# One weight load of 128 rows, or eight loads of 16 rows each: the first transfer of a decode attention kernel

## The chip, the cores and the metric

The kernel runs on one core of a Trainium2 chip. The metric is the device time of one execution in microseconds (us). A core has a matrix engine (PE), a vector engine (DVE), a scalar engine (ACT), GpSimd (POOL) and a sync engine (SP), which work at the same time and wait for one another through semaphores. Data comes from the chip's main memory into the 128 rows (partitions) of the core's own memory through 16 DMA engines; SP and ACT each issue transfers into a queue of their own, and both queues are served by the same 16 DMA engines.

## The reference

```python
def _A_ref(x, k_cache, v_cache, wq, wo):          # B = 2, H = 16, Sk = 4096, Dh = 256, D = 448, all float32
    q = (x @ wq).reshape(B, Sq, H, Dh).transpose(0, 2, 1, 3)
    scores = einsum("bhqd,bhkd->bhqk", q, k_cache) * (Dh ** -0.5)
    p = softmax(scores)
    o = einsum("bhqk,bhkd->bhqd", p, v_cache)
    return o.transpose(0, 2, 1, 3).reshape(B, Sq, H * Dh) @ wo

def _B_ref(x, w1, b1, w2, b2):                    # D = 448, F = 1792
    h = x @ w1 + b1
    r = where(h > 0, h, 0)
    return (r * r) @ w2 + b2

g = sigmoid((x * gate_w).sum(-1, keepdims=True))
out = g * _A_ref(...) + (1 - g) * _B_ref(...)
```

One token for each of two sequences is decoded: attention over a cache of 4096 positions, a small feed-forward block beside it, and a gate that mixes the two. Nearly all the bytes are the two caches.

## The kernel before, in words

The work is cut into 16 rounds. A round is one sequence and two heads: a K tile and a V tile of 128 rows with 64 KB in each row. The two K tiles `kp0` and `kp1` are used in turn, and `vp` holds the V tile. For a round DVE multiplies K by the query, broadcast over the positions (`times_q`, L438), and sums each product (`row_sums`, L443); a maximum, the exponentials on ACT and the products with V on PE (`values`) follow. Rounds 0 to 11 run in hardware loops on PE, the last four are written out.

Every transfer goes through the helper `load` (L270), which gives it a semaphore by name and tells the flow which stretch of which tile it writes. The flow derives the waits from these stretches: a reader waits for the semaphores of the transfers that wrote what it reads. SP issues all large loads, in the order of the program text; an issue that has to wait for a buffer holds up everything behind it on SP.

The start matters here. SP issues, in this order: `wq` into the front of `vp` (L299), the K tile of round 0 (`load_k(0)`, L398), and then, once PE has read `wq`, `w1` into the same place, and the K tile of round 1. ACT issues four small loads (x, gate_w, b2, and b1 as 16 rows). When `wq` has landed, PE makes all the queries with `times_x` (56 matrix products into `po1`), ACT scales them into `qs`, PE and ACT spread the first two over the rows (`make_q`), and DVE can begin its first `times_q` when the K tile of round 0 is there as well. `wq` lies in memory so that each of the 128 rows of the tile gets one contiguous stretch of 57,344 bytes:

```python
wq_t = vp[:, :D * N // P]
load(SP, "wq", wq_t, wq.rearrange(by7, k=XR, s=2).rearrange("(p k) n -> p (k n)", k=XR), [place(vp, 0, D * N // P)])
```

## Time and profile before

| what | value |
|---|---|
| median of 3 runs | 677.41 us (677.40 to 677.64) |
| the profiled execution's own time | 677.56 us |
| its span, from the first to the last instruction | 676.2 us |
| DVE busy | 571.2 us (84% of the span) |
| PE busy | 251.1 us (37%) |
| bytes moved by DMA | 289.73 MB, 428 GB/s over the span |
| packets of SP's queue | 6624, which took 99.2% of the 16 DMA engines' time |

The times of single steps come from the profiled execution, counted from the start of its span; 1.36 us of its own time lie outside the span. It was 0.15 us above the median of the three runs, whose own spread is 0.24 us. In the stretches of the profile a packet's bytes are booked where the packet starts, so a stretch of a microsecond or two can show more than the engines can move or nothing at all; only long stretches give a rate.

### The profile page before, as it was taken

Reading aid. Unit: us, or ns where it says so; the run is one execution under the profiler, and the core shown is the slowest. Engines: PE = TensorE matmul, PEld = TensorE weight load, DVE = VectorE, ACT = ScalarE, POOL = GpSimd, SP = SyncE. Lnnn points to the kernel's source line nnn. Section 1 sums busy time; section 2 is a strip of 40 time slices with the busy share of each in tenths; the row PEclk is TensorE's granted clock in tenths of the full one; section 3 lists DMA queues with packets and bytes.
Section 4 is the critical chain, followed back from the end, with each engine's and each line's share of the span. In section 5 each row is a group of like instructions: output and inputs, shape, how many; then the busy total and the mean of one; then the engine's idle time right before and its main releaser. Section 6 shows DMA issues by size and latency. Waiting matters only on the chain.

```text
span 676.2 us, 3914 instructions
## 1 busy us (share of the span) xinstructions
PE 251.1 (37%) x1716; PEld 86.2 (13%) x1716; DVE 571.2 (84%) x147; ACT 43.0 (6%) x143; POOL 0.7 (0%) x6
## 2 busy tenths in 40 slices
PE   2612350402305751140505455050411480411597
PEld 1100210100001510010101411010100140100123
DVE  3069999999999895979979896897979899999930
ACT  0001000000100201010000201000010110000000
POOL 0000000000000000000000000000000000000000
PEclk9956585665758567585856578575575856565889
DMA  9999999999999999999999999999999999999997
GB/s 381 434 430 435 435 434 434 434 434 435 434 434 434 439 435 426 430 434 434 434 430 434 450 435 434 434 434 430 430 434 430 403 462 434 434 431 430 400 435 308
DMA packets 6695, 289.73 MB, mean 428 GB/s; under 512 B 790, under 2 KB 924, under 8 KB 1564
## 3 DMA queue, kind: packets, MB, share of 16 engines
q1 hardware_dynamic: 6624, 289.54, 99.2%
q8 instruction: 9, 0.15, 0.1%
q10 hardware_dynamic: 60, 0.02, 0.0%
q14 instruction: 2, 0.02, 0.0%
HBM read 289.56 MB, written 0.01 MB: 428 GB/s over the span
## 4 chain that ended last, share of the span: by engine, by line
DMA 43%; DVE 26%; PE 3%; SPq 0%; issue 0%; DVEq 0%
DMA kp<-in_A_k_cache_dram 26%; DVE s L443 13%; DVE kp L438 13%; DMA vp<-in_A_v_cache_dram 11%; DMA kp<-in_B_w_dram 6%; PE po L362 3%; SPq L270 0%; PE fin L362 0%; PE mt L362 0%; DVE shared L727 0%; DVE nb L465 0%; DVEq L155 0%
## 5 line engine op out<-in xcount | busy, mean ns | idle before, releaser
L438 DVE TENSOR_TENSOR kp<-kp,q 128x8192 f32<-128x8192 f32 (+2 forms) x34 | 278.2, 8183 | 49.4 <-DMA kp<-in_A_k_cache_dram 49.3
L443 DVE TENSOR_REDUCE s<-kp 128x32 f32<-128x8192 f32 x32 | 277.9, 8686 | 1.1
L362 PE MATMUL po<-vp,pw 128*16 128x512 f32 (+1 forms) x960 | 134.9, 724 | 229.5 <-PEq L153 208.7
L362 PEld LDWEIGHTS po<-vp,pw 128*16 128x16 f32 (+1 forms) x960 | 31.0, 110 | 330.1 <-issue 306.4
L362 PE MATMUL mt<-ident,m 128*64 128x64 f32 x64 | 7.3, 318 | 142.2 <-PEq L153 88.1
L362 PE MATMUL sm<-rl,shared 128*128 128x8 f32 (+1 forms) x120 | 24.4, 340 | 9.4 <-ACT shared L523 8.1
L362 PE MATMUL acc<-wo,oTw 128*2 128x448 f32 x48 | 24.8, 683 | 2.5 <-ACT oTw L532 2.5
L362 PEld LDWEIGHTS sm<-rl,shared 128*128 128x128 f32 x120 | 23.8, 303 | 11.6 <-DVE rl L496 4.6
L362 PEld LDWEIGHTS mt<-ident,m 128*64 128x64 f32 x64 | 4.8, 192 | 156.0 <-issue 99.8
L484 ACT ACTIVATE pw<-zero 128x128 f32<-128x128 f32 x12 | 3.7, 311 | 324.5 <-PE po L362 324.5
L472 ACT ACTIVATE pw<-s,nb 64x64 f32<-64x64 f32 x32 | 11.1, 348 | 169.8 <-DVE nb L465 169.6
L727 DVE COPY shared<-fin 128x112 f32<-128x112 f32 x1 | 0.3, 275 | 20.1 <-PE fin L362 20.1
L362 PE MATMUL po<-kp,pw 128*8 128x512 f32 x64 | 9.9, 779 | 6.9 <-DMA kp<-in_A_v_cache_dram 6.9
L362 PE MATMUL ph<-vp,xT 128*4 128x448 f32 x28 | 6.8, 648 | 15.3 <-DMA vp<-in_B_w_dram 15.3
L465 DVE TENSOR_REDUCE nb<-mt 128x1 f32<-128x64 f32 x16 | 3.6, 224 | 10.3 <-PE mt L362 10.3
L362 PE MATMUL pq<-qs,sel 128*64 128x256 f32 x48 | 12.3, 594 | 0.0
L362 PE MATMUL po<-vp,xT 128*4 128x512 f32 x56 | 9.1, 817 | 1.3 <-DMA vp<-in_A_wq_dram 1.3
L414 ACT ACTIVATE q<-pq 128x256 f32<-128x256 f32 x16 | 6.1, 384 | 21.6 <-PE pq L362 21.3
L494 DVE RECIPROCAL rc<-sm 128x8 f32<-128x8 f32 (+1 forms) x5 | 1.0, 196 | 7.7 <-PE sm L362 7.7
L523 ACT ACTIVATE shared<-po 128x512 f32<-128x512 f32 x12 | 6.5, 592 | 11.4 <-PE sm L362 11.4
L362 PEld LDWEIGHTS acc<-wo,oTw 128*2 128x2 f32 x48 | 4.5, 98 | 20.5 <-issue 17.8
L362 PE MATMUL ph<-kp,ones_pp 128*16 128x512 f32 x48 | 6.7, 593 | 0.0
(77 smaller groups left out, 77.2 us busy)
## 6 DMA issues: line engine op xcount, KB each, us to landing
vp<-in_A_wq_dram SPq DMA_DIRECT2D x1, 7168.0 KB, 19.7
wo<-in_A_wo_dram SPq DMA_DIRECT2D x3, 1792.0 KB, 46.5
vp<-in_A_v_cache_dram SPq DMA_DIRECT2D x1, 4096.0 KB, 24.2
vp<-in_B_w_dram SPq DMA_DIRECT2D x1, 3136.0 KB, 17.6
vp<-in_A_v_cache_dram SPq DMA_DIRECT2D x1, 3072.0 KB, 31.1
wo<-in_A_wo_dram SPq DMA_DIRECT2D x2, 896.0 KB, 33.9
kp<-in_B_w_dram SPq DMA_DIRECT2D x1, 1792.0 KB, 36.9
vp<-in_A_v_cache_dram SPq DMA_DIRECT2D x1, 1024.0 KB, 33.1
```

What stands on the lines that cost most here:

```text
L362: i = t_.matmul(out_, lhsT, rhs, start=start, stop=stop, skip_group_check=True)
L414: op(ACT, lambda: s_.activation(t, pq[:, :DH], AF.Copy), r=["pq"], w=[f"q{i % 3}"])
L438: vec(lambda: v_.tensor_tensor(kt, kt, q.unsqueeze(1).to_broadcast([P, hi - lo, DH]), op=ALU.mult), at + [f"q{i % 3}"], at)
L443: vec(lambda: v_.tensor_reduce(s[:, at], rows(t)[:, at, :], axis=AX.X, op=ALU.add), [place(t, half * HALF, (half + 1) * HALF)], [(f"s{i % ...
L465: vec(lambda: v_.tensor_reduce(nb, mt[:, :PH], axis=AX.X, op=ALU.max, negate=True), ["mt"], [f"nb{i % 2}"])
L472: op(ACT, lambda: s_.activation(pw[at, :, 2 * c:2 * c + 2], s[at].rearrange("p (m s) -> p m s", s=2), AF.Exp, bias=nb[at], accum_out=rs[at ...
L484: op(ACT, lambda: s_.activation(at, zero.unsqueeze(2).unsqueeze(3).to_broadcast([P, NK // 2, 2, 2]), AF.Copy), r=["zero"], w=[("pw0", 2 * ...
L494: vec(lambda: v_.reciprocal(c, sm[:, :B * n].rearrange("p (k b) -> p k b", b=B)), ["sm"], ["rc"])
L523: op(ACT, lambda s=s, lo=lo: s_.activation(o_w[:, s], pv[:, s, lo:lo + HJ // 2].unsqueeze(2).to_broadcast([P, HJ // 2, HG, HP]), AF.Copy), ...
L727: vec(lambda: v_.tensor_copy(y4, fin[:, :DQ]), ["fin"], [("shared", 0, DQ)])
```

## The change

The one load of `wq` becomes eight. Load number r (0 to 7) takes the rows r, r + 8, r + 16 and so on, 16 rows of 57,344 bytes. All eight count up one semaphore, `wq`, and the matrix products that read `wq` wait once, for the count of all eight. What each load writes is now kept under a name of its own (`wq0` to `wq7`), and the products still read the stretch of `vp` too, so `w1`, which goes into the same stretch, is still held back until they are done. The bytes, their place in the tile, the order of everything else on SP, and the products are the same.

```diff
+    WQ_STEP = 8
...
     by7 = "(r k) (s n) -> (r k s) n"
     wq_t = vp[:, :D * N // P]
-    load(SP, "wq", wq_t, wq.rearrange(by7, k=XR, s=2).rearrange("(p k) n -> p (k n)", k=XR), [place(vp, 0, D * N // P)])
+    wq_v = wq.rearrange(by7, k=XR, s=2).rearrange("(p k) n -> p (k n)", k=XR)
+    for r in range(WQ_STEP):
+        load(SP, "wq", wq_t[r:P:WQ_STEP, :], wq_v[r:P:WQ_STEP, :], [f"wq{r}"])
+    wq_at = [f"wq{r}" for r in range(WQ_STEP)] + [place(vp, 0, D * N // P)]
...
-    op(PE, times_x(po_t[1], wq_t, QB, NQ // 2), r=["xT", place(vp, 0, D * N // P)], w=["po1"])
+    op(PE, times_x(po_t[1], wq_t, QB, NQ // 2), r=["xT", *wq_at], w=["po1"])
```

## The prediction

> **What bounds the kernel now.** I read the slices first, then the queues, the chain, and last the rows of the first 60 us.

> ```profile
> DVE  3069999999999895979979896897979899999930
> PEclk9956585665758567585856578575575856565889
> DMA  9999999999999999999999999999999999999997
> GB/s 381 434 430 435 435 434 434 434 434 435 434 434 434 439 435 426 430 434 434 434 430 434 450 435 434 434 434 430 430 434 430 403 462 434 434 431 430 400 435 308
> q1 hardware_dynamic: 6624, 289.54, 99.2%
> DMA 43%; DVE 26%; PE 3%; SPq 0%; issue 0%; DVEq 0%
> ```

> The DMA engines are busy in every slice and move 434 GB/s in nearly all of them, whether wq, K, V or wo is on its way. SP's queue fills 99.2% of the time of the 16 engines. DVE has high shares too, but the chain gives 43% to DMA and 26% to DVE: DVE frees a K tile, the next loads queue behind what is already in flight, and DVE waits for them again. Long stretches of the middle say the same:

> ```profile
> 200.00:300.00 100.00, 45.16 (x258) 16.32 (x258) 89.11 (x18) 7.21 (x24) 0.00 (x0) 0.69 1.01 435
> 300.00:400.00 100.00, 38.10 (x202) 14.93 (x202) 89.80 (x21) 8.37 (x29) 0.00 (x0) 0.61 1.00 431
> 400.00:500.00 100.00, 30.57 (x216) 7.92 (x216) 87.00 (x16) 4.29 (x17) 0.00 (x0) 0.65 1.01 436
> ```

> The last two columns are the DMA share and GB/s: the queue has no gap in which a delay made at the start could be taken back, nor one into which time won there would vanish. Whatever the change does to the moment at which the first K tile has landed, it does to the end. So the question is only how long wq keeps the 16 engines. What happens there:

> ```profile
> 0.74 0.39 SPq L270 DMA_DIRECT2D vp<-in_A_wq_dram  x1
> 1.19 0.41 SPq L270 DMA_DIRECT2D kp<-in_A_k_cache_dram  x1
> 20.46 9.08 PE L362 MATMUL po<-vp,xT 128*4 128x512 f32 x56 [1.35 <-DMA vp<-in_A_wq_dram]
> 29.62 0.33 SPq L270 DMA_DIRECT2D vp<-in_B_w_dram  x1
> 32.11 0.38 ACT L414 ACTIVATE q<-pq 128x256 f32<-128x256 f32 x1 [0.75 <-PE pq L362]
> 39.87 8.69 DVE L438 TENSOR_TENSOR kp<-kp,q 128x8192 f32<-128x8192 f32 x1 [20.14 <-DMA kp<-in_A_k_cache_dram]
> vp<-in_A_wq_dram SPq DMA_DIRECT2D x1, 7168.0 KB, 19.7
> ```

> SP issues wq at 0.74 and the K tile right behind it. wq lands at 20.4, 19.7 us after its issue. The queries are ready at 32.49 (32.11 + 0.38), and DVE starts at 39.87, released by the K tile and not by the queries.

> **The data of wq, the term that decides.** 7168 KB are 7.340 MB; at 434 GB/s they take 16.91 us. One row is 56 KB, and one of 16 engines moves 434/16 = 27.1 GB/s, so a row takes one engine 2.12 us, eight rows one after the other. The short stretches show these waves (bytes are booked where a packet starts):

> ```profile
> 0.00:1.70 1.70, 0.00 (x0) 0.00 (x0) 0.71 (x3) 0.00 (x0) 0.70 (x6) 1.00 0.00 0
> 1.70:2.70 1.00, 0.00 (x0) 0.00 (x0) 0.94 (x3) 0.43 (x1) 0.00 (x0) 1.00 2.64 921
> 2.70:4.30 1.60, 0.00 (x0) 0.00 (x0) 1.56 (x10) 0.85 (x1) 0.00 (x0) 1.00 0.00 0
> 4.30:5.10 0.80, 0.12 (x1) 0.12 (x1) 0.63 (x3) 0.00 (x0) 0.00 (x0) 1.00 2.66 1147
> 5.10:6.40 1.30, 1.30 (x7) 1.30 (x7) 0.00 (x0) 0.00 (x0) 0.00 (x0) 1.00 0.00 0
> 6.40:7.20 0.80, 0.45 (x3) 0.36 (x2) 0.24 (x2) 0.00 (x0) 0.00 (x0) 1.00 2.68 1159
> ```

> Sixteen rows start between 1.7 and 2.7 (921 GB/s for 1 us is 16 times 57,344 bytes), the next sixteen from 4.3 on, the next from 6.4 on. So each engine works on one row at a time, and there is always one row of wq on each engine. The change keeps that: how a small transfer is spread can be counted in the first 20 us.

> ```profile
> q1 hardware_dynamic: 160, 8.39, 99.3%
> q10 hardware_dynamic: 44, 0.02, 0.5%
> ```

> ACT's queue, q10, has four loads in this stretch, three of 2 rows and b1 of 16 rows. If every engine in use gets one data packet and one closing packet, that makes 3 x 4 + 32 = 44, which is what is there. SP's queue has 128 rows of wq, 16 closing packets, and the first 16 rows of K: 160. A transfer of 16 rows therefore runs on all 16 engines with one row on each, and so will each of the eight.

> What changes is which sixteen rows are written at the same time. Before, the hardware divides 128 rows among the engines as it likes; afterwards the rows in flight together are r, r + 8, ..., r + 120. Whether these sixteen can be written at full speed no row of the trace shows, because every other large load has 128 rows. The bounds: at best the rate stays, 16.91 us. On the other side, if the rows go into the memory over paths that each serve several rows, and two of the sixteen share one, each engine gets half of its 27.1 GB/s: 4.23 us a row, 33.8 us for wq, +16.91 us. Four rows to a path would make it +50.7 us.

> I take the pairs, +16.91. The nearest evidence is the ceiling itself: 434 GB/s whether the source rows are K's 64 KB or wq's 56 KB, in all kinds of company, is a limit of fixed paths on the core's side rather than of the source, and rows at a regular distance of 8 are a narrow choice of rows. The trace fits that but doesn't prove it, hence the chances below.

> [...]

> **Seven more issues on SP, and the start.** The rows for issues that follow one another, and for the shortest one:

> ```profile
> 631.98 1.29 SPq L270 DMA_DIRECT2D vp<-in_A_v_cache_dram  x3
> 633.31 8.01 SPq L270 DMA_DIRECT2D kp<-in_B_w_dram  x4
> 1.33 0.25 ACTq L270 DMA_DIRECT2D kp<-in_gate_w_dram  x1
> ```

> Three issues in a row take 1.29 us, 0.43 each. Seven more move the K issue from 1.19 to about 4.2 (7 x 0.43 = 3.0). K's first rows are needed when wq's last have gone, near 19; 14 us of queued wq hide this, and without that cover it would cost the 3.0. Nor does an engine wait for its next row: load r is issued by about 0.74 + 0.43 r, and its wave begins at about 1.7 + 2.1 r at the earliest. In the tail four issues took 8.01 us, so SP can be held up by a long queue; but there, three pieces of V and several earlier loads lay ahead of them, and here at most eight closing packets per engine are added to eight rows. I count nothing.

> A smaller first load can only start sooner. The bounds: its issue may take 0.25 us in place of 0.39 (0.14), and the first wave took from 1.7 to 4.3, 2.6 in place of 2.1 us (0.5 if an engine no longer waits for other rows' descriptors). So 0 to 0.64 us are won; I take 0.3, because the first rows also have to come a first time.

> Each engine closes eight loads in place of one: seven packets more. ACT's 44 packets took 0.5% of 16 x 20 us, 36 ns each, with the small data packets among them: 0 to 0.25 us, I take 0.1, that is, nearer to the rows where a large packet follows at once.

> **Waits.** There is no new one. The eight loads share a semaphore, PE waits once, and ACT's and SP's own waits stay. What PE does behind wq is hidden now: queries are ready 7.4 us before DVE is released by K (32.49 against 39.87), and w1, issued at 29.62, has 10 us until K has left the queue. If wq is late, K is late by the same amount, so both covers move along. b1 and its product stand before the wq products in PE's order:

> ```profile
> 18.35 0.77 PE L362 MATMUL ph<-kp 16*128 16x112 f32 x2 [2.63 <-DMA kp<-in_B_b_dram]
> L362 PE MATMUL po<-vp,xT x56: 592/787/1057, 20.5 to 29.0; 128*4 128x512 f32 x56
> ```

> b1 is released at 18.35 between wq's packets; with waves twice as long it is there by 1.7 + 2 x 16.65 = 35.0 at the latest, and wq by 20.4 + 16.9 = 37.3: still in front. A lower clock would stretch the 56 products: the same product takes 592 to 1057 ns, so 9.08 us would become at most 9.08 x 1057/787 = 12.2, 3.1 more, inside the 7.4.

> **The sum.** In the profiled execution 677.56 + 16.91 - 0.3 + 0.1 = 694.3. It lay 0.15 above the median of the runs, which gives 694.1; since the gain at the start is uncertain where the first wave itself is slowed, I leave the two small terms out: 677.41 + 16.91 = 694.3. The case's own range has as its ends -1.0 (the 0.64, and some 0.4 of overlap where waves of different loads meet) and +1.2 (closings 0.25, and up to half of a 2.12 us row lost where the last wave passes over to K): 693.3 to 695.5. The smallest difference that a measurement of this kernel can tell from none I put at 0.2%, 1.35 us.

> **The rivals.** First, not slower: the order in flight is the old one. If an engine already worked through eight neighbouring rows, engine e on 8e to 8e + 7, then the sixteen rows in flight were always r, r + 8, ..., and the change repeats them exactly; or the paths serve any sixteen rows alike. For it speaks that the engines' 2.1 us per row stays the same through all eight waves; against it that nothing shows which rows these are. Its price is the start and the closings alone: 677.41 - 0.3 + 0.1 = 677.2, between 676.8 (-0.64) and 677.7 (+0.25). It decides from the second wave on: if that begins by 4.3 and the third 2.1 us later, this is the case. Chance 0.26, nearly all of it within 0.2%, for 0.64 is less than 1.35; 0.04 of it for a gain larger than any row suggests.

> Second, the pair shares unevenly: one engine of a pair runs at full rate through its first four rows (8.46 us) and the other is held back; then, if rows 4 to 7 of a block have other paths than rows 0 to 3, they no longer meet. The cost is half, 8.46 us: 685.9. For it speaks that the engines are not in step now (the starts of a wave are spread over about a microsecond); against it, that the spread stays that small and no engine gets ahead. Chance 0.07.

> Third, four rows to a path: 677.4 + 50.7 = 728.1. Against it: the sixteen rows are spread over the whole memory, from r to r + 120. Chance 0.03.

> Fourth, the change doesn't do what it says: a load of 16 rows uses fewer engines. The count of b1's packets speaks against it. With half of the engines and full rate, wq would take twice as long too, 694.3, unless loads run side by side. Chance 0.02, slower.

> **How the numbers follow.** Pairs at half rate 0.62, uneven 0.07, four to a path 0.03, fewer engines 0.02: slower by over 0.2% 0.74. No collision 0.26, of which 0.22 within 0.2% and 0.04 faster. The likeliest case gives 694.3. Its own range holds only about 0.6, so the range has to reach to the other end, the case without collision, whose low end is 676.8; I put 676.7 and 695.5, and the uneven case lies inside.

> **What would show it.** If I am right, the windows of the first 40 us show waves every 4.2 us in place of 2.1, about 217 GB/s over the stretch of wq, wq landing near 37, DVE's first multiplication near 56.8 in place of 39.87, and from there the same 434 GB/s and the same chain, shifted by 17 us. SP's issues of wq would still be 0.4 us apart. PE would reach its wait for wq later, behind b1, and lose nothing of its own. I am wrong if the third wave starts at 6.4 as before: then rows eight apart don't meet, and only the start counts. I am wrong in another way if wq takes 34 us but DVE starts less than 16 us later, or if a gap in the DMA row swallows part of it.

## The result, and the profile after

The changed kernel takes 696.60 us (median of 5 runs, 696.35 to 696.84) against 677.41 for the kernel before (5 runs beside it, 677.40 to 677.67): ratio 1.0282, 95% interval 1.0270 to 1.0293, or 19.2 us more. The forecast was 694.3 within 676.7 to 695.5. The direction and the halved rate came out; the size lies 1.1 us above the range.

The profiled execution of the changed kernel took 696.60 us, with a span of 695.2. First the slices and queues of its page:

```profile
DVE  3006999999999899697979899597979989999930
DMA  9989999999999999999999999999999999999997
GB/s 212 211 362 426 442 453 426 422 430 427 456 434 426 409 459 434 430 422 434 437 445 430 405 444 453 430 426 434 430 445 434 430 423 441 437 423 434 407 434 312
q1 hardware_dynamic: 6736, 289.54, 99.2%
DMA 42%; DVE 25%; PE 3%; SPq 0%; issue 0%; DVEq 0%
```

The bytes are the same; 112 packets are new (7 on each of 16 engines, as many as seven more closings each). The DMA engines are as busy as before, but in the first two slices (17.4 us each) they move 212 and 211 GB/s where 381 and 434 stood. From the fourth slice on the rate is the old one, and the shares of the chain are nearly the same. Now the first steps, from the order of time, and the waves of wq (us, busy time of the engines, clock, DMA share, GB/s in the last column):

```profile
0.73 5.08 SPq L271 DMA_DIRECT2D vp<-in_A_wq_dram  x8
5.86 0.58 SPq L271 DMA_DIRECT2D kp<-in_A_k_cache_dram  x1
13.22 0.76 PE L366 MATMUL ph<-kp 16*128 16x112 f32 x2 [1.47 <-DMA kp<-in_B_b_dram]
39.47 8.23 PE L366 MATMUL po<-vp,xT 128*4 128x512 f32 x56 [25.49 <-DMA vp<-in_A_wq_dram]
50.25 0.38 ACT L418 ACTIVATE q<-pq 128x256 f32<-128x256 f32 x1 [0.75 <-PE pq L366]
58.78 8.69 DVE L442 TENSOR_TENSOR kp<-kp,q 128x8192 f32<-128x8192 f32 x1 [44.19 <-DMA kp<-in_A_k_cache_dram]
```

```profile
0.00:2.10 2.10, 0.00 (x0) 0.00 (x0) 1.11 (x3) 0.00 (x0) 0.70 (x6) 1.00 0.01 2
2.10:5.50 3.40, 0.53 (x3) 0.53 (x3) 2.72 (x13) 1.28 (x1) 0.00 (x0) 1.00 1.26 270
10.00:14.50 4.50, 2.52 (x5) 0.66 (x5) 0.61 (x3) 0.00 (x0) 0.00 (x0) 1.00 1.00 206
14.50:19.00 4.50, 0.00 (x0) 0.00 (x0) 0.10 (x1) 0.00 (x0) 0.00 (x0) 1.00 0.99 204
19.00:23.30 4.30, 0.00 (x0) 0.00 (x0) 0.00 (x0) 0.00 (x0) 0.00 (x0) 1.00 1.00 213
23.30:27.80 4.50, 0.00 (x0) 0.00 (x0) 0.00 (x0) 0.00 (x0) 0.00 (x0) 1.00 1.00 204
32.30:36.80 4.50, 0.00 (x0) 0.00 (x0) 0.00 (x0) 0.00 (x0) 0.00 (x0) 1.00 0.99 204
40.00:57.00 17.00, 9.00 (x64) 1.78 (x56) 0.00 (x0) 1.36 (x3) 0.00 (x0) 0.91 1.00 432
```

Each of these waves is sixteen rows, and it now takes 4.3 to 4.5 us in place of 2.1 (the packets themselves: 2.116 us before; after, a median of 4.43 to 4.47 in six of the eight waves and 4.29 in the first and the fifth), although the DMA share is full. wq is there at 39.47 in place of 20.46, DVE starts at 58.78 in place of 39.87: 18.9 us later. The end of the span is 19.0 later. So all of the loss arises while wq is on its way, and none of it is taken back: the queries are ready at 50.63, 8.2 us before DVE can use them.

### The profile page after: what moved, and what is told of

Same layout as the page of the kernel before. It is cut to its first block, busy times and chain, and to the rows that moved or that the text cites. A ratio compares the mean times of both kernels' runs of the same rounds, so it can differ in the third digit from the quotient of the medians.

```text
span 695.2 us, 3921 instructions
## 1 busy us (share of the span) xinstructions
PE 253.3 (36%) x1716; PEld 86.6 (12%) x1716; DVE 571.2 (82%) x147; ACT 42.9 (6%) x143; POOL 0.7 (0%) x6
## 3 DMA queue, kind: packets, MB, share of 16 engines
q1 hardware_dynamic: 6736, 289.54, 99.2%
## 4 chain that ended last, share of the span: by engine, by line
DMA 42%; DVE 25%; PE 3%; SPq 0%; issue 0%; DVEq 0%
DMA kp<-in_A_k_cache_dram 26%; DVE s L447 13%; DVE kp L442 12%; DMA vp<-in_A_v_cache_dram 11%; DMA kp<-in_B_w_dram 6%; PE po L366 3%; SPq L271 0%; PE fin L366 0%; PE mt L366 0%; DVE shared L731 0%; DVE nb L469 0%; DVEq L155 0%
## 5 line engine op out<-in xcount | busy, mean ns | idle before, releaser
L366 PE MATMUL po<-vp,pw 128*16 128x512 f32 (+1 forms) x960 | 136.7, 733 | 228.2 <-PEq L153 206.5
L366 PE MATMUL acc<-wo,oTw 128*2 128x448 f32 x48 | 25.6, 702 | 2.5 <-ACT oTw L536 2.5
L366 PE MATMUL po<-vp,xT 128*4 128x512 f32 x56 | 8.2, 751 | 25.5 <-DMA vp<-in_A_wq_dram 25.5
L418 ACT ACTIVATE q<-pq 128x256 f32<-128x256 f32 x16 | 6.1, 383 | 20.7 <-PE pq L366 20.4
## 6 DMA issues: line engine op xcount, KB each, us to landing
wo<-in_A_wo_dram SPq DMA_DIRECT2D x2, 896.0 KB, 33.9
vp<-in_A_v_cache_dram SPq DMA_DIRECT2D x1, 1024.0 KB, 33.9
```

What stands on the lines that cost most here:

```text
L366: i = t_.matmul(out_, lhsT, rhs, start=start, stop=stop, skip_group_check=True)
L418: op(ACT, lambda: s_.activation(t, pq[:, :DH], AF.Copy), r=["pq"], w=[f"q{i % 3}"])
```

## The experiments

The theory on trial is a supposition: the 128 rows are written over 16 paths, and a path carries about what one engine can bring, so that two engines on one path each run at half rate. No record names a path; whether there are such groups of rows, and which rows are in one, only the rates below can say. The rivals: every load costs something of its own; the source rows, 448 KB apart, are read slowly; loads of 16 rows are slow whatever their rows. The experiments keep all else as in the change and replace its loop of loads.

**Eight loads of all rows, an eighth of the columns in each.**

```diff
-        load(SP, "wq", wq_t[r:P:WQ_STEP, :], wq_v[r:P:WQ_STEP, :], [f"wq{r}"])
+        load(SP, "wq", wq_t[:, r * WL:(r + 1) * WL], wq_v[:, r * WL:(r + 1) * WL], [f"wq{r}"])    # WL = 1792
```

> Eight loads of wq as in the change, with the same bytes and the same issues on SP, but each takes all 128 rows and an eighth of their columns (7,168 bytes of each row). Shared write paths (the rows in flight decide): as fast as the kernel before, 677.4 within 1 us, wq landed near 20.5, first DVE multiplication near 40. Number of loads (every load costs something of its own): as slow as the change, near 696.

677.96 us against 677.61, ratio 1.0005 (0.9996 to 1.0014). From its order of time:

```profile
0.74 4.22 SPq L271 DMA_DIRECT2D vp<-in_A_wq_dram  x8
40.14 8.69 DVE L443 TENSOR_TENSOR kp<-kp,q 128x8192 f32<-128x8192 f32 x1 [27.83 <-DMA kp<-in_A_k_cache_dram]
```

Eight issues take SP 4.22 us and DVE starts 0.27 later than before: the number of loads, their size of 896 KB and the later issue of K together cost a few tenths of a microsecond.

**Sixteen neighbouring rows in a load.**

```diff
-        load(SP, "wq", wq_t[r:P:WQ_STEP, :], wq_v[r:P:WQ_STEP, :], [f"wq{r}"])
+        load(SP, "wq", wq_t[r * WB:(r + 1) * WB, :], wq_v[r * WB:(r + 1) * WB, :], [f"wq{r}"])    # WB = 16
```

> Eight loads of 16 rows, but of 16 neighbouring rows each (16r to 16r + 15). [...] Number of loads: as the change, 696. Source rows too far apart: the sixteen source rows in flight are now neighbours, so about 677.

725.69 us, ratio 1.0708 (1.0691 to 1.0724), +48.1. Three of its waves, in windows:

```profile
16.30:24.50 8.20, 1.65 (x2) 0.08 (x2) 0.00 (x0) 0.00 (x0) 0.00 (x0) 1.00 1.01 113
24.50:32.60 8.10, 0.77 (x2) 0.50 (x2) 0.54 (x2) 0.00 (x0) 0.00 (x0) 1.00 1.01 113
32.60:40.80 8.20, 0.00 (x0) 0.00 (x0) 0.00 (x0) 0.00 (x0) 0.00 (x0) 1.00 1.00 112
```

A wave takes 8.16 us, nearly four times the 2.12. Same bytes, same number of loads, and source rows side by side, which should have helped if their distance were the cause: which rows are written together decides. The price is that of four rows to a path, a little under the 728.1 us that the prediction's third rival puts on it. An estimate from these rates, with four paths here and eight in the change: 112.5/4 = 28.1 GB/s for each of the four, against 204/8 = 25.5 for each of the eight, so that four engines on a path do not lose what a pair loses.

**The rows of the change, read from neighbouring source rows.**

```diff
-        load(SP, "wq", wq_t[r:P:WQ_STEP, :], wq_v[r:P:WQ_STEP, :], [f"wq{r}"])
+        load(SP, "wq", wq_t[r:P:WQ_STEP, :], wq_v[r * WB:(r + 1) * WB, :], [f"wq{r}"])
```

> The eight loads of the change write the same rows r, r + 8, ..., but read sixteen neighbouring source rows each (16r to 16r + 15), so wq lies in the tile in another order and the queries come out of permuted weights. Shared write paths alone: as the change, 4.47 us a row, 696.6. The distance of the source rows alone: 677. If pairs halve the rate and the source distance adds the 6% by which a row was slower than half rate (4.47 against 4.23): 4.23 us a row, 694.5.

696.16 us, ratio 1.0274 (1.0258 to 1.0290), rows of 4.25 to 4.47 us after the first wave, as in the change. One wave:

```profile
23.45:27.95 4.50, 0.00 (x0) 0.00 (x0) 0.00 (x0) 0.00 (x0) 0.00 (x0) 1.00 0.99 204
```

The source has no part in it that can be told (the time is 0.4 us below the change's), neither in the half rate nor in the 6% beyond it.

**Two loads, rows 0 to 63 and 64 to 127.**

```diff
-    for r in range(WQ_STEP):
-        load(SP, "wq", wq_t[r:P:WQ_STEP, :], wq_v[r:P:WQ_STEP, :], [f"wq{r}"])
+    for r in range(2):
+        load(SP, "wq", wq_t[r * PH:(r + 1) * PH, :], wq_v[r * PH:(r + 1) * PH, :], [f"wq{r}"])    # PH = 64
```

> Two loads of wq, rows 0 to 63 and rows 64 to 127. Shared write paths: each half reaches 8 of 16 paths, 4.2 to 4.5 us a row, 694 to 697. Number of loads: an eighth of the change's effect or less, 678 to 680. Small loads of 16 rows being slow in themselves: 677.

696.56 us, ratio 1.0281 (1.0265 to 1.0297). Two loads cost as much as eight, with rows of 4.25 to 4.48 us. One wave:

```profile
14.70:19.20 4.50, 0.00 (x0) 0.00 (x0) 0.00 (x0) 0.00 (x0) 0.00 (x0) 1.00 1.00 205
```

A load of 3.5 MiB to one half of the rows gave 205 GB/s in its steady waves against 434 before: a ratio of 0.47, a little below one half.

**Four loads of 32 rows, and two of 64, spread over the whole memory.**

```diff
+    for r in range(4):
+        load(SP, "wq", wq_t[r:P:4, :], wq_v[r:P:4, :], [f"wq{r}"])     # the other kernel: range(2), r:P:2
```

> Four loads of 32 rows, every fourth row in one (r, r + 4, ...). Each load reaches all 16 paths with two rows each, and every engine gets two rows. Shared write paths, engines dealt neighbouring entries of the list (rows r + 8e, then r + 8e + 4): the sixteen rows in flight are again eight apart, 4.47 us a row, 696. Shared write paths, engines dealt one path each, as the full rate of the 128-row load suggests: 2.12 us a row, 677.5. What counts is the paths that a load reaches as a whole, whatever is in flight: 677.5.

> Two loads of 64 rows, every second row in one (r, r + 2, ...). All 16 paths with four rows each, four rows for every engine. Engines dealt neighbouring entries (rows r + 8e, + 2, + 4, + 6): rows in flight eight apart again, 4.47 us a row, 696. Engines dealt one path each, or only the reach of the whole load counting: 677.5.

678.01 and 678.10 us, ratios 1.0005 (0.9996 to 1.0015) and 1.0006 (0.9996 to 1.0015). The second to fourth wave of the loads of 32 rows:

```profile
4.80:6.95 2.15, 1.86 (x8) 1.77 (x8) 0.13 (x1) 0.00 (x0) 0.00 (x0) 1.00 1.00 428
6.95:9.10 2.15, 0.00 (x0) 0.00 (x0) 1.47 (x9) 0.20 (x1) 0.00 (x0) 1.00 1.01 431
9.10:11.25 2.15, 1.64 (x4) 0.58 (x4) 0.35 (x3) 0.00 (x0) 0.00 (x0) 1.00 0.99 427
```

A load needn't have 128 rows: these two ran at full rate, 427 to 431 GB/s in these waves and 428 to 430 in the same ones of the loads of 64 rows. If the rows in flight decide, their rows were also dealt to the engines so that those in flight didn't meet, for dealing neighbouring entries would have put r + 8e together again and cost the 4.47 us a row of the change. The runs show the rate; the dealing is inferred from it.

**Sixteen rows with fewer meetings.**

```diff
+    for r in range(7):
+        load(SP, "wq", wq_t[r:r + 106:7, :], wq_v[r:r + 106:7, :], [f"wq{r}"])
+    load(SP, "wq", wq_t[112:P, :], wq_v[112:P, :], ["wq7"])
```

> Seven loads of 16 rows, every seventh row in one (r to r + 105), and one load of the rows 112 to 127. Shared write paths: in a load only two to four of sixteen rows meet another on their path, so most engines go on at 2.1 us a row and get out of step; worked out path by path, the slowest engine takes 25.4 to 26.2 us (the last load, four rows to a path, is most of the loss), +8.5 to +9.3: 686 to 687. Loads of 16 rows slow whatever their rows: 696.

695.68 us, ratio 1.0264 (1.0247 to 1.0281): a miss of 9 us. Its waves, one window each from load 2 to load 7:

```profile
5.70:9.94 4.24, 2.24 (x9) 1.64 (x9) 1.72 (x10) 0.20 (x1) 0.00 (x0) 1.00 1.00 217
9.94:14.10 4.16, 1.83 (x4) 0.49 (x2) 0.54 (x2) 0.00 (x0) 0.00 (x0) 1.00 1.02 222
14.10:17.12 3.02, 0.00 (x0) 0.00 (x0) 0.00 (x0) 0.00 (x0) 0.00 (x0) 1.00 0.96 304
17.12:20.06 2.94, 0.00 (x0) 0.00 (x0) 0.00 (x0) 0.00 (x0) 0.00 (x0) 1.00 1.05 312
20.06:23.68 3.62, 0.00 (x0) 0.00 (x0) 0.00 (x0) 0.00 (x0) 0.00 (x0) 1.00 1.09 253
23.68:27.80 4.12, 0.00 (x0) 0.00 (x0) 0.00 (x0) 0.00 (x0) 0.00 (x0) 1.00 1.02 223
```

Which rows share a path can be worked out from the rates. Sixteen groups of eight rows, the four rows 4m to 4m + 3 and the four that lie 32 away in the same half of the memory, put four rows in flight on a path in the blocks (8.16 us a row), two in the change (4.43 to 4.47) and in the pairs close to each other (4.47, below), and one in the loads of 8 rows without pairs (2.12, below). One half of the memory has eight of the sixteen groups, and went at half rate (205 GB/s). Of all groupings by four of the seven bits of the row number this is the only one that gives these rates; it is a fit to them, and no record shows a path itself.

By this grouping, loads 1 to 3, 6 and 7 have two pairs of rows on a shared path, loads 4 and 5 one pair. The waves follow it: 3.6 to 4.2 us with two pairs (loads 2, 3, 6 and 7), about 3 with one. But the twelve rows that by the grouping meet nobody were slow as well: in load 3 all sixteen packets took 4.00 to 4.19 us; in load 4 two took 4.21 and 4.22 and the rest 2.39 to 3.01. So by the grouping a crowded path held up the other engines too. That the engines work independently of one another was the wrong part of this expectation; through what they are coupled, none of the runs shows.

**Pairs of rows close to each other.**

```diff
+        lo, hi = 32 * (r // 2) + r % 2, 32 * (r // 2 + 1)
+        load(SP, "wq", wq_t[lo:hi:2, :], wq_v[lo:hi:2, :], [f"wq{r}"])
```

> Eight loads of 16 rows, every second row of a block of 32 (0, 2, ..., 30 first). Again eight paths with two rows each, but the two that meet are two rows apart and not 32 apart as in the change. The extra 6% (4.47 us a row against twice 2.116 = 4.23) due to the distance of the two rows on a path: 4.08 (half of the 8.156 that four neighbouring rows took) to 4.23 us, 693.1 to 694.3. Due to two engines sharing, whatever the rows: 4.47, 696.5.

696.78 us, ratio 1.0283 (1.0266 to 1.0300), again 4.47 us a row. One wave:

```profile
23.70:28.20 4.50, 0.00 (x0) 0.00 (x0) 0.00 (x0) 0.00 (x0) 0.00 (x0) 1.00 1.00 204
```

Whether the two rows that share a path by the grouping lie 2 apart, as here, or 32, as in the change, makes no difference to the 6%: 4.47 us against 4.43 to 4.47.

**Loads of 8 rows: four pairs, and no pair.**

```diff
+    for r in range(16):
+        load(SP, "wq", wq_t[r:P:16, :], wq_v[r:P:16, :], [f"wq{r}"])       # four pairs
...
+        lo, hi = 32 * (r // 4) + r % 4, 32 * (r // 4 + 1)
+        load(SP, "wq", wq_t[lo:hi:4, :], wq_v[lo:hi:4, :], [f"wq{r}"])     # no pair
```

> Sixteen loads of 8 rows, every sixteenth row in one (r, r + 16, ...), so that eight engines work and their rows meet in four pairs, in place of sixteen engines and eight pairs. The 6% by which a pair was slower than half rate belongs to any two engines on one path: 4.47 us a row, 16 rows one after the other 71.5 us, +54.6, about 732. It belongs to eight pairs at once: 4.1 to 4.25 us a row, 66 to 68 us, +49 to +51, about 727. If loads of 8 rows were dealt to other engines in turn, half of these times or less.

> Sixteen loads of 8 rows, every fourth row of a block of 32 (0, 4, ..., 28 first), so that each of the eight rows has a path of its own. Shared write paths: 2.12 us a row although the load is smaller than any of the others, 16 rows on each of eight engines 33.9 us, +16.9, about 694.5; engines dealt in turn: 677.5. Small loads slow in themselves: 4.2 us a row or more, +51 and over.

746.46 us (ratio 1.1017, 1.0985 to 1.1049) and 710.51 us (1.0486, 1.0456 to 1.0517), the first above every expected time, the second between two of them (694.5 for shared paths, some 728 for small loads slow in themselves). The windows of the kernel without pairs show why:

```profile
4.60:6.80 2.20, 1.82 (x8) 1.78 (x8) 0.32 (x2) 0.00 (x0) 0.00 (x0) 1.00 0.51 213
9.00:11.20 2.20, 2.20 (x5) 0.69 (x6) 0.16 (x1) 0.00 (x0) 0.00 (x0) 1.00 0.48 209
13.30:20.20 6.90, 0.00 (x0) 0.00 (x0) 0.00 (x0) 0.00 (x0) 0.00 (x0) 1.00 1.13 427
20.20:46.10 25.90, 0.00 (x0) 0.00 (x0) 0.00 (x0) 0.00 (x0) 0.00 (x0) 1.00 1.00 207
52.40:72.20 19.80, 9.78 (x64) 1.94 (x64) 0.00 (x0) 1.36 (x3) 0.00 (x0) 0.80 0.73 306
```

At first half of the engines work (share 0.5) and bring 209 to 213 GB/s, 2.12 us a row: these loads of only 8 rows, none of which meet by the grouping, ran at full rate per engine. At 13.8 the first rows of K, issued at 11.64, start on the eight idle engines. While wq writes rows 0 to 63, both together move 427 by the window; a share of 1.13 says that rows which end later are counted in, and at a share of 1 it is 378. From 20.2 on wq writes rows 64 to 127, and now all 16 engines together move 207: wq's rows take 4.45 us, K's 64 KB rows 5.1 in place of 2.42, until those eight engines are done with K. Then wq is back at 2.12 us. From this it is inferred that K's rows on those engines were rows 64 to 127, and that rows of different loads meet on a path just as rows of one load do; no record names the row that an engine writes. The rest of the extra time is K itself, whose other half still had to go through the engines that wq had kept (0.73 of DMA share from 52.4 to 72.2).

In the kernel with pairs a load of wq by the grouping uses four paths, two of them for rows from 64 on, and only on these two a third row, one of K's, can join. Yet in loads 6 and 7 all eight rows of wq took 6.35 us, three times 2.12 (5.1 to 6.4 over loads 3 to 11), and all eight rows of K beside them 7.2 to 7.3, three times 2.42:

```profile
33.00:39.30 6.30, 0.00 (x0) 0.00 (x0) 0.00 (x0) 0.00 (x0) 0.00 (x0) 1.00 0.73 105
```

At a share of 1 the 105 GB/s are 144, a third of 434: every engine went at the pace that three rows on one path would give, as in the step of seven every engine was near the pace of a pair (4.00 to 4.19 us in load 3). Before K starts and after its share is done there, wq's rows take 4.40 to 4.47 us (loads 2, 14 and 15): with four pairs the loss beyond half rate is 4 to 6%, about that of eight pairs.

**A step of five rows.**

```diff
+    for r in range(15):
+        lo = 40 * (r // 5) + r % 5
+        load(SP, "wq", wq_t[lo:lo + 36:5, :], wq_v[lo:lo + 36:5, :], [f"wq{r}"])
+    load(SP, "wq", wq_t[120:P, :], wq_v[120:P, :], ["wq15"])
```

> Fifteen loads of 8 rows, every fifth row of a block of 40, and one of the rows 120 to 127. Worked out by the bits of the row number, loads 1 to 5 and 11 to 15 have one or two pairs on a path among their eight rows, loads 6 to 10 none. If only the rows that meet are slow, the other four to six rows of a load keep 2.12 us. If a crowded path holds up every engine (as the step of seven suggested, where two pairs slowed all sixteen to 4.15 and one pair the rest to 2.4 to 3.0), the other rows of loads 1 to 5 and 11 to 15 take 2.4 to 4.2 us, and those of loads 6 to 10 are back at 2.12. In time 705 to 722, with the last load, four rows to a path, near 8.2 us of it.

726.01 us, ratio 1.0715 (1.0684 to 1.0746), above the range. Here too K was under way on the other engines, from 12.5 us on. In the middle of the loads without pairs all engines together moved about half of 434:

```profile
20.00:37.00 17.00, 0.00 (x0) 0.00 (x0) 0.00 (x0) 0.00 (x0) 0.00 (x0) 1.00 1.04 216
```

By the grouping loads 6 to 9 have no pair of their own, and only three of their eight rows lie from 64 on, where K's rows, as inferred above, were being written; the other five share no path with any row of K or of their own load. Still all eight rows of each took 4.1 to 4.4 us. In the kernel of 8 rows without pairs, where wq wrote rows 0 to 63 and no row met another, wq's rows took 2.1 to 2.7 us beside K. So by the grouping this run too has engines held up by crowded paths that they don't use. What a single pair does it leaves open: in load 2, before K came, four rows kept 2.12 us while two others took 3.40 and 4.04.

**The rows of the change, cut in two.**

```diff
+    for r in range(16):
+        cut = slice(r % 2 * WL, (r % 2 + 1) * WL)                          # WL = 7168 elements
+        load(SP, "wq", wq_t[r // 2:P:WQ_STEP, cut], wq_v[r // 2:P:WQ_STEP, cut], [f"wq{r}"])
```

> The rows of the change, each cut in two: sixteen loads of 16 rows of 28,672 bytes. The loss beyond half rate (4.47 us a row in place of 4.23) is a rate: 2.24 us for half a row, and the change's time, 696.6. It is a fixed cost of every row (0.24 us, as when an engine passes from one row to the next): 2.12 + 0.24 = 2.36 us for half a row, 1.9 us more than the change, 698.5.

696.28 us, ratio 1.0276 (1.0258 to 1.0293); half a row takes about 2.24 us. One wave:

```profile
25.98:28.22 2.24, 0.00 (x0) 0.00 (x0) 0.00 (x0) 0.00 (x0) 0.00 (x0) 1.00 1.01 205
```

The loss beyond half rate is a lower rate (205 GB/s, as with whole rows) and not a cost of each row.

## Why the prediction was right or wrong

The deciding step held as far as rates can show it: the rows in flight together are r, r + 8, ..., and the rate fell by about half, from 434 GB/s to 204 to 206 in nearly all steady waves. That they meet two by two on paths is the grouping's reading of it. The loads that differ only in which rows are written together (neighbouring rows 725.7 us, every eighth row 696.6, every fourth or second row 678.0 and 678.1) rule the rivals out: the order in flight was not the old one, the number of loads costs nothing that can be told (677.96 for eight loads of columns), and no engine stays unused. The uneven pair didn't come about either: wave after wave the sixteen rows kept together.

What failed is the size of that term. It was worked out as exactly half of 434 GB/s: 33.8 us for wq, +16.91. No run shows it: the loads with pairs got 204 to 206 GB/s in all steady waves but one, by the grouping 25.6 GB/s for two engines together where one alone gets 27.1. With 205, wq takes 7.340 MB / 205 = 35.8 us, +18.9, which is the 18.9 us by which DVE starts later. The range allowed +1.2 on top for closings and the passage to K, but it took the half for a bound: nothing was left for two engines getting less out of a path than one. Nor is the ceiling of 434 GB/s shown to be a limit of paths: eight engines at work alone, on eight rows without a pair, went at 2.12 us a row, 27.1 GB/s each, so sixteen at their own pace make 434 as well. Source, distance of the two rows and row length are not the reason, and with four pairs in place of eight the loss is nearly the same. It is not constant either: the fifth wave, from about 19.2 to 23.5 us, took 4.29 us a row in the change and 4.25 to 4.26 with neighbouring source rows, halves and near pairs. Why it is so stays open.

The small terms: the start was to win 0.3 us and won nothing; the smaller first load did not start sooner. The first rows start at 2.16 in place of 1.77 (nothing but 2 GB/s until 2.10 in the window), and an issue took 0.63 us on SP (5.08/8) in place of the 0.43 reckoned with. K is issued at 5.86 and not at 4.2, which the queued wq hid as said, by a wide margin. b1 came at 13.2, far ahead of its bound of 35.0 and ahead of the 18.35 of before, although the rows were slower. With rows as slow and two loads in place of eight (the halves) it came at 25.4. That each closing of a load gives its packets a turn would fit, but isn't shown. The cover behind wq held, 8.2 us. That the shift passes through whole held best: +18.9 at DVE's start, +19.0 at the end of the span, and in the kernel with neighbouring rows +48.1 both at DVE's start (88.01) and in the time.

The chances put 0.62 on pairs at half rate, the case nearest to what came. The error was in the size: the range's upper end rested on a bound for a thing that the trace had never shown, two engines on one path.

## What to carry to other kernels

If a load is cut by rows, try pieces that take rows from all over the memory: loads of 32 rows, every fourth one, and of 64, every second one, ran at full rate here (427 to 431 GB/s), while rows eight apart, 16 neighbouring rows and one half of the memory got 204 to 206, 112 to 113 and 205, a factor of two to four. Cutting by columns cost a few tenths of a microsecond (DVE's start 0.27 later). In this kernel, with the 16 DMA engines at work for 99.2% of the time, the 18.9 us lost at the start were 19.0 at the end. A load of 8 rows used half of the engines and let the next one start beside it, at 13.8 us, and from 20.2 us on both ran at half rate together (207 GB/s): look for rows of two loads that can meet. And a few rows that meet can slow a whole load, not only themselves (4.00 to 4.19 us for all sixteen rows with two pairs among them).
